# Attention on one core: probabilities transposed on TensorE, or a second score product with keys stationary

## Chip, core and metric

The kernel runs on one core of a Trainium2 chip. The metric is the device time of one execution in microseconds (us). The engines are TensorE (PE, with its weight loads listed as PEld), VectorE (DVE), ScalarE (ACT), GpSimd (POOL) and SyncE (SP), which issues nearly all transfers. Every engine takes its instructions in the order of its own list and waits at an instruction until what it needs is there.

## The reference, cut to what matters

```python
def _A_ref(x, wq, wk, wv, wo, beta):      # S = 2048, D = 1024, 32 heads of 32
    ...                                   # q, k, v: 4 segments of L = 512 rows
    for s in range(N):
        logits = jnp.einsum("bhqd,bhkd->bhqk", qs, ks) * scale + mask    # causal in a segment
        p = _softmax(logits, axis=-1)
        a_dot = jnp.einsum("bhqk,bhkd->bhqd", p, vs)
        num = jnp.einsum("bhld,bhde->bhle", pq, M)       # pq = phi(qs)
        den = jnp.einsum("bhld,bhd->bhl", pq, z)[..., None] + 1e-6
        o = g * num / den + (1.0 - g) * a_dot            # g = sigmoid(beta), by head
        M = M + jnp.einsum("bhld,bhle->bhde", pk, vs)    # pk = phi(ks)
        z = z + jnp.einsum("bhld->bhd", pk)
    return o @ wo
h = x + _A_ref(_layernorm(x), wq, wk, wv, wo, beta)
h2 = h + _B_ref(_layernorm(h), w1, b1, w2, b2)           # layernorm, dense, gelu, dense
```

## The kernel before, in words

All products keep near full single precision by splitting each factor into a high part, which TensorE multiplies in one pass, and a low part (`x = xh + xl`); three products `ah*bh + ah*bl + al*bh` make one (`mm3`, lines 124 to 126). A score product needs only one instruction, because the three blocks of 32 rows (high, low, high of the keys against high, high, low of the queries) lie under each other in a stack of 96 rows (`ks`, `qs`), which SP puts together by transfers (`stack`).

The program treats two halves of 1024 rows one after the other: attention with its three projections, then the product with `wo`, then the dense block. In a half there are two segments and eight groups of four heads. A **unit** is one group in one segment: `dense` projects keys, queries and values in 24 steps of three matmuls. Meanwhile `heads` treats the four heads of the unit before, six steps to a head; `interleave` takes the two in turn, one step each. 28 of the 32 units are in the steady stretch that the prediction speaks of.

What a head does at which step stands in the table `HEAD`: the number is the step, counted from the head's start (a head is 6 steps behind the one before it), the fraction orders what falls on the same step. `TIMES` does the same for the unit's own side work. This is the order in which the code is written out. A scheduler then makes each engine's list from it: it may move an instruction of lower rank ahead of one whose inputs or buffers it takes to be not yet ready. The lists below are its result.

For one head before:

- `qk`: four score products with a block of 128 queries stationary and 128, 256, 384 or 512 keys moving (`pqk`, line 659). DVE adds the mask, scales and takes the row's extreme in the same instruction, into `pr` and `mx` (line 660). ACT takes the exponential in place with the row's sum (line 668).
- `ptr`: ten transposes of 128x128 turn the probabilities so that keys lie on partitions (`ppt`, line 709), in groups of four, four and two. ACT makes the high part `pth` from each group (line 711), DVE the low part `ptl` (`sub`, line 716).
- `av`: eight products with 64 columns of values stationary, the high and low part of `v` side by side (`po`, line 729). ACT copies the low half out (`ot`, line 734), DVE adds the high half (line 740).
- `inverse` and `weigh`: reciprocals of the row sums, times 1 - g, for four heads at once; they are transposed (`pw`, line 688) and spread over partitions through DRAM (`r_dram`). POOL multiplies (`w`, line 743) and adds what the memory gave (line 747).

The banks of PSUM are shared out: two for scores (`qk`), two for transposed probabilities (`pt`), one for `po` (`av`), three for projections and the memory's products (`d`). POOL also makes the low parts of the weights (`wl`, line 799) and of `pk` and `pq`.

Of the kernel before, what the change touches and what calls it, by code (L numbers as in the profile page):

```python
# [17 lines left out]
P = 128  # L18
# [11 lines left out]
RA, RH, RS, PD, PS = 1.3, 14, 0.7, 20, 3  # L30
VT, KT, OT = True, True, True
WLC = 8
TIMES = dict(pk=10, kx=12, pkh=21, pkl=22, ks=11, qs=16, pq=16, pqh=20, pql=20, omt=20, vx=24, pm=25, vs=32, vl=33, pmm=40, om=35, omc=40, od=62, lk=13, lq=16, lv=20, ck=18, cq=22, cv=28)
HEAD = dict(r=6.1, q0=1.1, a0=14.1, s2=14.2, t0=8.3, q2=2.4, s0=8.5, a1=15.1, q1=3.2, t1=10.1, w=9.2, q3=4.3, t2=11.1, o=17.2, s1=11.3)
# [13 lines left out]
def build(tc, x, wq, wk, wv, wo, beta, w1, b1, w2, b2, out):  # L48
# [13 lines left out]
    hsel = const.tile([P, 76], F32, name="hsel")[:, 0:4]  # L62
# [6 lines left out]
    gate = const.tile([P, 2, H], F32, name="gate")  # L69
    bb = const.tile([P, H], F32, name="bb")  # L70
# [3 lines left out]
    def constants():  # L74
# [3 lines left out]
        nc.scalar.activation(gate[:, 1, :], gate[:, 0, :], AF.Identity, scale=-1.0, bias=1.0)  # L78
        pb = ps_dense("pb")
# [12 lines left out]
    r_dram = [dram.tile([16, P], F32, name=f"r_dram{k}") for k in range(2)]  # L92
# [260 lines left out]
    def attention(half, first):  # L353
# [6 lines left out]

        scr = [acts["zt"].tile([P, 4, 512], F32, tag=f"t{x_}3", name=f"sc{x_}") for x_ in "hl"]
# [31 lines left out]
        def stack(a, b, name, order):  # L393
            out = []
            n = acts[name] = acts.get(name, 0) + 1
            d = s_dram[name][n % 2]
            direct = {"ks": KD, "qs": QD}[name]
            for j in range(4):
                st = ab.tile([96, 512], F32R, tag=name, name=name, bufs=5)
                out.append(st)  # L400
                if j < direct:
                    for blk, src in enumerate(order):
                        nc.sync.dma_start(raw(st).rearrange("(r b) n -> b r n", b=3)[blk], raw((a, b)[src][32 * j:32 * j + 32, :]))
            if direct < 4:
                for blk, src in enumerate(order):
                    nc.sync.dma_start(d[32 * direct:, blk], raw((a, b)[src])[32 * direct:])
            for j in range(direct, 4):
                nc.sync.dma_start(raw(out[j]), d[32 * j:32 * j + 32].rearrange("r b n -> (r b) n"))
# [23 lines left out]
        def dense(g, sl, ws, u):  # L432
# [12 lines left out]
            vs = u["vs"] = ab.tile([P, 16, 64], F32R, name="vs", bufs=2)  # L445
# [11 lines left out]
            def key_stack():  # L457
                u["ks"] = stack(v["kh"], v["kl"], "ks", (0, 1, 0))
# [37 lines left out]
            def query_stack():  # L496
                u["qs"] = stack(v["qh"], v["ql"], "qs", (0, 0, 1))
# [183 lines left out]
        def weigh(st):  # L681
            u, j = st["u"], st["j"]
            if j < 3:
                return
# [917 lines left out]
```

## Time and profile before

| | |
|---|---|
| median of 3 runs | 2275.07 us (2273.71 to 2276.27) |
| span of the profiled execution | 2272.7 us |
| PE busy | 2243.7 us, 99% |
| DVE, ACT, POOL busy | 68%, 54%, 38% |
| attention and projections, first half | about 40 to 490 us of the span |
| the same, second half | about 900 to 1380 us |

The profiled execution is one run; its span goes from the first to the last instruction, and the median of the times is 2.4 us above that span. A row of the timeline gives the start, the duration, the engine, the line, the operation and the operands, and in brackets the idle time ahead of it. On PE, matmuls overlap: what one costs is the distance to the start of the next, not its duration. A row of the groups gives the count, then busy time and mean ns of one, then idle time before. In the source view the three numbers are the least, the median and the largest duration in ns. A row of the windows gives the stretch, its length, then the busy time (and count) of PE, PEld, DVE, ACT and POOL, the granted TensorE clock, the share of the DMA engines and GB/s.

### The profile page before, as it was taken

Reading aid. Unit: us, or ns where it says so; the run is one execution under the profiler, and the core shown is the slowest. Engines: PE = TensorE matmul, PEld = TensorE weight load, DVE = VectorE, ACT = ScalarE, POOL = GpSimd, SP = SyncE. Lnnn points to the kernel's source line nnn. Section 1 sums busy time; section 2 is a strip of 40 time slices with the busy share of each in tenths; the row PEclk is TensorE's granted clock in tenths of the full one; section 3 lists DMA queues with packets and bytes.
Section 4 is the critical chain, followed back from the end, with each engine's and each line's share of the span. In section 5 each row is a group of like instructions: output and inputs, shape, how many; then the busy total and the mean of one; then the engine's idle time right before and its main releaser. Section 6 shows DMA issues by size and latency. Waiting matters only on the chain.

```text
span 2272.7 us, 34849 instructions
## 1 busy us (share of the span) xinstructions
PE 2243.7 (99%) x11481; PEld 1861.9 (82%) x11481; DVE 1541.0 (68%) x3073; ACT 1232.8 (54%) x2553; POOL 856.8 (38%) x710
## 2 busy tenths in 40 slices
PE   8999999999999999999999999999999999999999
PEld 6888888877888888888888887888888888888887
DVE  6777777776656565777777787655666766567653
ACT  6777777774453445777777775453334223222221
POOL 4232233334244442233333334244445654055430
PEclk9999999999999999999999999999999999999999
DMA  6666666665475655666655565466568975476762
GB/s 215 182 190 181 181 179 176 177 177 196 139 212 165 189 167 173 195 177 179 178 173 169 178 195 189 142 210 181 162 177 310 331 253 197 155 257 226 244 234 89
DMA packets 400798, 437.41 MB, mean 192 GB/s; under 512 B 33102, under 2 KB 267114, under 8 KB 400618
## 3 DMA queue, kind: packets, MB, share of 16 engines
q1 hardware_dynamic: 337450, 398.48, 56.8%
q10 hardware_dynamic: 63168, 36.71, 5.4%
q8 instruction: 91, 1.49, 0.3%
q14 instruction: 89, 0.73, 0.1%
HBM read 287.41 MB, written 128.78 MB: 183 GB/s over the span
## 4 chain that ended last, share of the span: by engine, by line
PE 86%; DMA 4%; POOL 3%; ACT 2%; DVE 2%; issue 1%; SPq 1%; POOLq 0%; ACTq 0%; DVEq 0%
PE po L1436 22%; PE bps L1040 10%; PE cps L1040 7%; PE dps L1040 7%; PE po L729 6%; PE ppt L709 5%; PE pqk L659 3%; PE qps L124 3%; PE qps L125 2%; PE kps L124 2%; PE qps L126 2%; PE vps L124 2%; PE kps L126 2%; PE kps L125 2%; PE vps L125 2%; PE vps L126 2%
## 5 line engine op out<-in xcount | busy, mean ns | idle before, releaser
L668 ACT ACTIVATE pr<-pr,mx 128x128 f32<-128x128 f32 (+3 forms) x512 | 289.1, 565 | 107.3 <-DVE mx L660 104.0
L660 DVE CUSTOM_DVE_ANT_0 pr<-pqk,mask 128x128 f32<-128x128 f32 (+3 forms) x512 | 247.2, 484 | 87.0 <-PE pqk L659 82.2
L711 ACT CAST pth<-ppt 128x512 fp32r<-128x512 f32 (+1 forms) x384 | 194.9, 512 | 91.3 <-PE ppt L709 88.9
L716 DVE TENSOR_TENSOR ptl<-ppt,pth 128x512 fp32r<-128x512 f32 (+1 forms) x384 | 226.8, 595 | 14.5 <-ACT pth L711 11.9
L709 PE MATMUL ppt<-ident,pr 128*128 128x128 f32 x1280 | 217.4, 276 | 0.7 <-DVE ptl L716 0.4
L1446 DVE TENSOR_TENSOR c<-c,po 128x512 f32<-128x512 f32 x160 | 105.4, 683 | 149.0 <-PE po L1436 147.2
L709 PEld LDWEIGHTS ppt<-ident,pr 128*128 128x128 f32 x1280 | 163.9, 140 | 36.7 <-issue 2.2
L659 PE MATMUL pqk<-ks,qs 96*128 96x128 f32 (+3 forms) x512 | 183.0, 358 | 1.1 <-DVE mx L660 1.1
L799 POOL TENSOR_TENSOR wl<-wr,wh 128x1024 fp32r<-128x1024 f32 x42 | 101.1, 2406 | 179.1 <-ACT wh L797 132.0
L729 PE MATMUL po<-ptl,vs 128*64 128x512 f32 (+3 forms) x512 | 153.1, 308 | 1.9 <-DVE ptl L716 1.9
L729 PE MATMUL po<-pth,vs 128*64 128x512 f32 (+3 forms) x512 | 147.8, 309 | 2.9 <-DVE ot L740 1.6
L1436 PE MATMUL po<-w2h,zh 128*128 128x512 f32 x378 | 121.0, 390 | 0.2 <-DVE zh L1376 0.2
L1040 PE MATMUL bps<-zh,sb 128*128 128x512 f32 x336 | 111.1, 391 | 0.0
L1293 POOL TENSOR_TENSOR w2r<-w2r 128x512 f32<-128x512 f32 x54 | 85.4, 1590 | 68.3 <-DMA w2r<-in_B_w 45.4
L1040 PE MATMUL bps<-zh,sa 128*128 128x512 f32 x336 | 110.9, 391 | 0.0
L124 PE MATMUL kps<-yh,wh 128*128 128x512 f32 (+1 forms) x264 | 109.9, 416 | 0.0
L124 PE MATMUL qps<-yh,wh 128*128 128x512 f32 x256 | 107.8, 421 | 0.0
L124 PE MATMUL vps<-yh,wh 128*128 128x512 f32 x256 | 106.2, 415 | 0.0
L659 PEld LDWEIGHTS pqk<-ks,qs 96*128 96x128 f32 x512 | 98.2, 192 | 8.3 <-DVE mx L660 1.8
L1436 PE MATMUL po<-w2h,hl 128*128 128x512 f32 x322 | 103.3, 390 | 0.4 <-DVE hl L1376 0.4
L125 PE MATMUL kps<-yl,wh 128*128 128x512 f32 (+1 forms) x264 | 102.8, 389 | 0.1
L126 PE MATMUL kps<-yh,wl 128*128 128x512 f32 (+1 forms) x264 | 102.9, 390 | 0.0
(251 smaller groups left out, 6527.8 us busy)
## 6 DMA issues: line engine op xcount, KB each, us to landing
hr<-h_dram SPq DMA_DIRECT2D x112, 448.0 KB, 5.3
w2r<-in_B_w SPq DMA_DIRECT2D x122, 256.0 KB, 4.3
r<-in_B_w SPq DMA_DIRECT2D x56, 512.0 KB, 4.5
ks<-ks_dram SPq DMA_DIRECT2D x128, 192.0 KB, 3.1
h_dram<-ht ACTq DMA_DIRECT2D x84, 256.0 KB, 3.7
ks_dram<-kh SPq DMA_DIRECT2D x64, 256.0 KB, 2.6
wr<-in_A_wo SPq DMA_DIRECT2D x32, 512.0 KB, 4.5
wx<-in_B_w SPq DMA_DIRECT2D x56, 256.0 KB, 3.5
```

The lines of the kernel that those rows point to most:

```text
L124: nc.tensor.matmul(ps, ah, bh, start=first, stop=False)
L125: nc.tensor.matmul(ps, ah, bl, start=False, stop=False)
L126: acts["mm"] = nc.tensor.matmul(ps, al, bh, start=False, stop=last)
L659: nc.tensor.matmul(pqk[:, :n], u["qs"][j][:, i * P:(i + 1) * P], u["ks"][j][:, 0:n], start=True, stop=True)
L660: nc.vector.tensor_tensor_reduce(out=st["pr"][:, offs[i]:offs[i] + n], in0=pqk[:, :n], in1=mask[:, 512 - n:512], op0=ALU.add, op1=ALU.min, ...
L668: nc.scalar.activation(pi, pi, AF.Exp, bias=mx[:, i:i + 1], scale=-1.0, accum_out=mx[:, 4 + i:5 + i])
L709: nc.tensor.transpose(ppt[:, o:o + P], pr[:, offs[i] + jk * P:offs[i] + (jk + 1) * P], ident)
L711: acts["pth"] = n, nc.scalar.copy(pth[:, base:base + w], ppt[:, :w])
L716: nc.vector.tensor_tensor(o, x0, x1, op=ALU.subtract)
L729: nc.tensor.matmul(po[:, P * jk:], v, st[part][:, koff[jk]:koff[jk] + w], start=(jk, part) == (0, "pth"), stop=(jk, part) == (2, "ptl"))
L1040: nc.tensor.matmul(ps, x_[:, c, :], y_[:, c, :], start=first and c == 0 and n == 0, stop=last and c == 3 and n == 2, skip_group_check=True)
L1436: nc.tensor.matmul(ps, x_[:, k], y_[k], start=opens and k == 0 and i == 0, stop=closes and k == self.KP - 1 and i == 2, skip_group_check=True)
```

## The change

The transposes go. The scores are computed twice: the first product is there for the row's maximum alone; the second has the keys stationary, so that its result has keys on partitions at once. The maximum is taken off inside that second product: the query stack gets two more rows with the high and the low part of the maximum, the key stack two rows of -1. The path of the maximum is: DVE writes it as two parts into `top`, transposes 32x32 blocks into `mt`, SP stores that in DRAM (`top_dram`) and loads two rows of 512 into the stack (`rows`). ACT takes the exponential out of PSUM (`again`, `pe<-psc`), POOL zeroes the masked part of the diagonal blocks (`affine_select`), ACT makes the high part (`upper`), DVE the low part of 1024 columns and POOL that of the last 256 (`lower`). The values get a column of ones, so that row 64 of `po` is the row's sum; it goes out by `os` and through DRAM (`sums_dram`, `r_dram`). The stacks become six fixed buffers, the pipeline goes from two slots behind to four, and the tables of steps are new.

```diff
-HEAD = dict(r=6.1, q0=1.1, a0=14.1, s2=14.2, t0=8.3, q2=2.4, s0=8.5, a1=15.1, q1=3.2, t1=10.1, w=9.2, q3=4.3, t2=11.1, o=17.2, s1=11.3)
+HEAD = dict(q0=0.3, q2=1.2, q1=2.3, q3=3.3, x=4.1, y=6.6, p0=9.2, p1=10.2, p2=11.2, h0=11.4, h1=12.4, l0=12.3, l1=13.1, a0=15.1, a1=16.1, r=16.9,
+            o=18.2, v=19.2, i=21.4, d=21.6, w=23.8, e=26.4)
+RING = 6
...
+        values = [ab.tile([P, 16, 72], F32R, name=f"vs{n}") for n in range(2)]
+        for t in values:
+            nc.gpsimd.memset(raw(t[:, :, 64:65]), 1.0)
...
         def qk(st, i):
-            nc.tensor.matmul(pqk[:, :n], u["qs"][j][:, i * P:(i + 1) * P], u["ks"][j][:, 0:n], start=True, stop=True)
+            nc.tensor.matmul(pqk[:, :n], u["qs"][j][0:96, i * P:(i + 1) * P], u["ks"][j][0:96, 0:n], start=True, stop=True)
             nc.vector.tensor_tensor_reduce(
-                out=st["pr"][:, offs[i]:offs[i] + n], in0=pqk[:, :n], in1=mask[:, 512 - n:512],
-                op0=ALU.add, op1=ALU.min, scale=-SCALE, scalar=3.0e38, accum_out=st["mx"][:, i:i + 1])
-            soft(st, i)
-        def soft(st, i):
-            nc.scalar.activation(pi, pi, AF.Exp, bias=mx[:, i:i + 1], scale=-1.0, accum_out=mx[:, 4 + i:5 + i])
+                out=pqk[:, :n], in0=pqk[:, :n], in1=mask[:, 512 - n:512],
+                op0=ALU.add, op1=ALU.max, scale=1.0, scalar=-3.0e38, accum_out=st["mx"][:, i:i + 1])
...
+        def largest(st):
+            nc.vector.tensor_copy(top[:, 0:4], st["mx"])
+            nc.vector.tensor_tensor(top[:, 4:8], st["mx"], raw(top[:, 0:4]), op=ALU.subtract)
+            nc.vector.transpose(mt, raw(top))
+            BQ.dma_start(top_dram[n].rearrange("(z a r) -> a z r", a=4, r=32), mt)
+        def rows(st):
+            BQ.dma_start(raw(st["u"]["qs"][st["j"]][96:98, :]), st["top"][0:8 * P].rearrange("(p n) -> p n", p=2))
+        groups = ((0,), (1, 3), (2,))
+        def again(st, n):
+            ps = psum.tile([P, 512], F32, tag="pt", name="psc", bufs=2)
+            for jk in grp:
+                m = 512 - P * jk
+                nc.tensor.matmul(ps[:, w:w + m], u["ks"][j][0:98, jk * P:(jk + 1) * P], u["qs"][j][0:98, P * jk:],
+                                 start=True, stop=True)
+            pe = st["pe"][:, base:base + w]
+            nc.scalar.activation(pe, ps[:, :w], AF.Exp, scale=SCALE)
+            nc.gpsimd.affine_select(d, d, pattern=[[0, k]] * (k > 1) + [[1, P]], compare_op=ALU.is_ge, fill=0.0,
+                                    base=0, channel_multiplier=-1)
+        pieces = (slice(0, 1024), slice(1024, 1280))
+        def upper(st, n):
+            nc.scalar.copy(st["pth"][:, pieces[n]], st["pe"][:, pieces[n]])
+        def lower(st, n):
+            (nc.gpsimd if n else nc.vector).tensor_tensor(st["ptl"][:, c], st["pe"][:, c], raw(st["pth"][:, c]), op=ALU.subtract)
-        def ptr(st, n):
-                    nc.tensor.transpose(ppt[:, o:o + P], pr[:, offs[i] + jk * P:offs[i] + (jk + 1) * P], ident)
-            acts["pth"] = n, nc.scalar.copy(pth[:, base:base + w], ppt[:, :w])
-        def sub(st, n):
-            nc.vector.tensor_tensor(o, x0, x1, op=ALU.subtract)
...
         def av(st, n):
-                v = u["vs"][:, 4 * j + jk, :]
+                v = u["vs"][:, 4 * j + jk, 0:65]
-                nc.scalar.copy(u["ot"][32 * j:32 * j + 32, :], po[32:64, :])
+                nc.scalar.copy(st["os"][0:65, :], po[0:65, :])
+        def spread(st):
+            BQ.dma_start(sums_dram[u["n"]][j:j + 1, :], st["os"][64:65, :])
...
```

The names in the lists: `vps` and `qps` are projections, `psc` is a second score product, `pqk` a first one, `po` a product with the values. First PE, at the products with the values of one head (`po`) in the middle of the first half. Before:

```order
L729 MATMUL po<-pth,vs 64x512
L729 MATMUL po<-ptl,vs 64x512
L729 MATMUL po<-pth,vs 64x384
L729 MATMUL po<-ptl,vs 64x384
L709 MATMUL ppt<-ident,pr 128x128 x4
L659 MATMUL pqk<-ks,qs 128x384
L124 MATMUL vps<-yh_437,wh 128x512
L125 MATMUL vps<-yl_438,wh 128x512
L126 MATMUL vps<-yh_437,wl 128x512
L729 MATMUL po<-pth,vs 64x128
```

And now, in the same stretch of the program; the `psc` and the `po` in it belong to the same head:

```order
L726 MATMUL psc<-qs_513,ks_450 128x512
L726 MATMUL psc<-qs_513,ks_450 128x384
L726 MATMUL psc<-qs_513,ks_450 128x128
L694 MATMUL pqk<-stacks 128x128
L726 MATMUL psc<-qs_513,ks_450 128x256
L694 MATMUL pqk<-stacks 128x384
L694 MATMUL pqk<-stacks 128x256
L694 MATMUL pqk<-stacks 128x512
L759 MATMUL po<-pth,vs_367 65x512
L759 MATMUL po<-ptl,vs_367 65x512
L759 MATMUL po<-pth,vs_367 65x384
L759 MATMUL po<-ptl,vs_367 65x384
```

Before, a piece of a head is followed by three matmuls of a projection, all the way through, and the last transposes of a head stand eleven rows or more ahead of its first `po`. Now a head's `po` stand right behind its own `psc`, with no projection between, and the four `psc` and eight `po` of the next head come next; the projections stand together elsewhere. Second POOL, ahead of that same place. Before:

```order
L513 TENSOR_TENSOR pql<-pq,pqh 128x512
L569 TENSOR_TENSOR MZ<-MZ,hsel 128x128
L475 TENSOR_TENSOR pkl<-scl,pkh 128x512
L509 CAST mzh<-MZ 128x132
L510 TENSOR_TENSOR mzl<-MZ,mzh 128x132
```

And now:

```order
L865 TENSOR_TENSOR wl<-wr,wh 128x1024 x2
L605 TENSOR_SCALAR MZ<-MZ,zc 128x1
L606 TENSOR_SCALAR MZ<-hsel,MZ 128x4
L808 TENSOR_TENSOR sch<-ot,sch 128x512
L812 TENSOR_TENSOR sch<-sch,omt 128x512
L733 AFFINE_SELECT pe<-pe 128x128
L733 AFFINE_SELECT pe<-pe 128x2x128
L733 AFFINE_SELECT pe<-pe 128x128
L746 TENSOR_TENSOR ptl<-pe,pth 128x256
L865 TENSOR_TENSOR wl<-wr,wh 128x1024
```

POOL now has steps of a head's own chain in its list (`pe`, `ptl`), and the other work of the unit (`wl`, `sch`) stands ahead of them.

172 lines of the change are left out of this document (101 added, 71 removed).

## The prediction

> **What bounds the kernel now.** I read the page first.
>
> ```profile
> span 2272.7 us, 34849 instructions
> PE 2243.7 (99%) x11481; PEld 1861.9 (82%) x11481; DVE 1541.0 (68%) x3073; ACT 1232.8 (54%) x2553; POOL 856.8 (38%) x710
> ```
>
> PE is busy nearly all the time, but its ends are modelled, so I asked the windows for the two steady stretches of attention, and the groups of the first stretch for the number of heads in it.
>
> ```profile
> 60.00:480.00 420.00, 419.80 (x2519) 352.51 (x2519) 319.83 (x907) 321.75 (x807) 127.16 (x134) 1.00 0.63 181
> 900.00:1340.00 440.00, 439.22 (x2617) 367.61 (x2616) 337.66 (x973) 334.68 (x837) 140.82 (x138) 1.00 0.61 178
> ...
> L668 ACT ACTIVATE pr<-pr,mx 128x512 f32<-128x512 f32 x56 | 40.7, 726 | 10.0 <-DVE mx L660 9.4
> ```
>
> PE idles 0.2 of 420 us and 0.8 of 440 us, at full clock; DVE and ACT are busy three quarters of the time, POOL a third. 56 heads in 420 us are 7.5 us a head, 60 us for eight (two units). So the stretch goes at the pace of TensorE's list. A change there pays what it takes out of that list, as long as PE never has to wait; and any wait that it puts into the list costs its full length. The third view is the timeline of PE, for the price of each piece.
>
> ```profile
> 301.02 0.33 PE L729 MATMUL po<-pth,vs 128*64 128x384 f32 x1
> 301.19 0.34 PE L729 MATMUL po<-ptl,vs 128*64 128x384 f32 x1
> 301.37 0.60 PE L709 MATMUL ppt<-ident,pr 128*128 128x128 f32 x4
> 301.72 0.42 PE L659 MATMUL pqk<-ks,qs 96*128 96x384 f32 x1
> 301.98 0.40 PE L124 MATMUL vps<-yh,wh 128*128 128x512 f32 x1
> 302.22 0.40 PE L125 MATMUL vps<-yl,wh 128*128 128x512 f32 x1
> ...
> 302.74 0.22 PE L729 MATMUL po<-ptl,vs 128*64 128x128 f32 x1
> 302.80 0.28 PE L729 MATMUL po<-pth,vs 128*64 128x256 f32 x1
> 302.92 0.28 PE L729 MATMUL po<-ptl,vs 128*64 128x256 f32 x1
> ...
> 303.86 0.60 PE L709 MATMUL ppt<-ident,pr 128*128 128x128 f32 x4
> 304.21 0.48 PE L659 MATMUL pqk<-ks,qs 96*128 96x512 f32 x1
> 304.53 0.40 PE L124 MATMUL vps<-yh,wh 128*128 128x512 f32 x1
> 304.76 0.40 PE L125 MATMUL vps<-yl,wh 128*128 128x512 f32 x1
> ...
> 305.22 0.38 PE L709 MATMUL ppt<-ident,pr 128*128 128x128 f32 x2
> 305.36 0.48 PE L124 MATMUL kps<-yh,wh 128*128 128x512 f32 x1
> 305.68 0.39 PE L125 MATMUL kps<-yl,wh 128*128 128x512 f32 x1
> ```
>
> From start to start, 512 moving columns cost 0.23 us, 384 cost 0.17, 256 cost 0.12, 128 cost 0.06.
>
> **What TensorE gains.** The ten transposes of a head cost 0.35 + 0.35 + 0.14 = 0.84 us, and the instruction behind each of the three groups starts its successor 0.09 us late (0.26 for 0.17, twice 0.32 for 0.23): 1.11 us in all. The four new products have the widths 512, 384, 256 and 128: 0.58 us. That is 0.53 us a head, 68 us over 128 heads, all of it on the path. Two more rows in the stack and a 65th value column change no moving width; I take them as free.
>
> **What TensorE waits for.** Before, the transposes of a head lie well ahead of its products with the values, with projections between. In the new list those products come close behind the second scores, and PE cannot go on to anything else. Between them lies a chain over three engines, priced by the nearest rows:
>
> ```profile
> L384 ACT ACTIVATE e<-kps x24: 578/598/607, 28.1 to 1301.0; 128x512 f32<-128x512 f32 x24
> L345 POOL TENSOR_SCALAR_AFFINE_SELECT mask<-mask x2: 292/293/294, 1.7 to 887.8; 128x128 f32<-128x128 f32 x2
> L797 ACT CAST wh<-wr 128x1024 fp32r<-128x1024 f32 x13 | 13.6, 1050 | 4.8 <-DMA wr<-in_A_wv 3.4 <-PE kps L125 1.4
> L101 DVE TENSOR_TENSOR wl<-wr,wh x9: 1176/1226/2136, 464.8 to 1427.4; 128x1024 fp32r<-128x1024 f32 x9
> ```
>
> The first score product is through after 0.40 us; two exponentials out of PSUM take 0.60 us each; the select on two diagonal blocks lies between 0.29 us (one block) and 0.59 (two), I take 0.45; then the high part of 1024 columns, 1.05 us. So the first `po` can start 3.1 us after the first `psc`, or 2.5 us after the second one where that comes late. The second `po` needs the low part, 1.23 us on.
>
> What lies between in the list covers the wait. Priced by the widths above, the first half repeats this every eight heads: 1.2, 0.4 (counted from the second `psc`), 2.2, 4.7, 1.2, 0.6, 2.1 and 2.8 us of other PE work. The first of these is the place shown with the change: four `psc` and four `pqk`, 1.16 us. The waits left are 1.9, 2.1, 0.9, 0, 1.9, 2.5, 1.0 and 0.3, together 10.6 us. Between first and second `po` stand 0.5, 0.3, 1.2, 0.3, 0.2, 0.2, 1.4 and 1.2 us against 1.23; where the fourth head's low part was long ready, that leaves 3.6 us. That makes 14.2 us for eight heads; the second half's cadence (1.2, 0.4, 2.2, 2.7, 0.9, 2.7, 2.7, 0.6) gives 13.7 in the same way. 14 us, times 14 such cycles (112 heads; those at the start of a half are spaced more widely): 196 us. An error of 0.5 us in the chain moves it by some 45 us either way.
>
> Two queues lengthen this chain.
>
> ```profile
> L743 POOL TENSOR_TENSOR sch<-ot,sch 128x512 f32<-128x512 f32 x7 | 9.1, 1299 | 7.1 <-DMA sch<-r_dram 4.8 <-DVE ot L740 2.3
> L747 POOL TENSOR_TENSOR sch<-sch,omt 128x512 f32<-128x512 f32 x7 | 9.2, 1319 | 0.5
> L660 DVE CUSTOM_DVE_ANT_0 pr<-pqk,mask 128x128 f32<-128x128 f32 (+3 forms) x512 | 247.2, 484 | 87.0 <-PE pqk L659 82.2
> L740 DVE TENSOR_TENSOR ot<-po,ot 32x512 f32<-32x512 f32 x57 | 38.7, 679 | 13.0 <-ACT ot L734 12.2
> ```
>
> On POOL the selects stand behind the unit's last multiply and add, 2.6 us that wait for a transfer: once in eight heads up to 2.6 us, or nothing if the transfer is early; I take 1. On DVE, once in eight heads the first products of four heads stand within 8.1 us of PE work, while their row maxima take 16 x 0.48 = 7.7 us and five operations like `ot` among them 3.4: about 3 us late, part of which lies in waits already counted; I take 2, between 0 and 5. Together 3 x 14 = 42 us. DVE's own load hardly changes: three low parts become one of 1.23 us, and three small operations on four columns come in. ACT loses four exponentials and gets three, so it has time. The low part now reads two SBUF tiles while POOL works: the row's largest, 2.14 us, bounds that. With it, the four heads per cycle that wait for the low part would lose 0.9 us each, 50 us in all. The Trainium skill (GPSIMD Engine Reference, Specifications) says that POOL shares its SBUF interfaces with VectorE and contends with DVE instructions of two SBUF inputs; by that rule the 50 us would come on top, 2530. The median in the row, taken beside a busy POOL, speaks for little of it.
>
> The pipeline's end is two slots longer; other work is there for PE, so I take 10 us, between 0 and 40.
>
> **The clock.** The one place of the trace where PE waits a little is the end of the first half:
>
> ```profile
> 488.00:491.50 3.50, 3.50 (x30) 3.16 (x29) 2.27 (x7) 1.64 (x4) 0.00 (x0) 1.00 0.75 227
> ...
> 509.40:512.80 3.40, 1.61 (x12) 0.98 (x10) 2.49 (x8) 3.35 (x8) 2.12 (x1) 1.00 0.03 7
> 512.80:516.30 3.50, 3.21 (x8) 2.54 (x9) 1.32 (x1) 0.12 (x2) 0.24 (x1) 0.51 0.56 154
> ...
> 511.24 0.45 PE L729 MATMUL po<-pth,vs 128*64 128x512 f32 x1 [0.91 <-DVE ot L740]
> ...
> 513.09 0.79 PE L125 MATMUL pwo<-zl,oh 128*128 128x512 f32 x1 [1.18 <-POOL zl L101]
> ```
>
> After 3.4 us with PE busy for 1.6, the next 3.5 us run at half clock, though no single gap was longer than 1.2 us. The new list has two such clusters in each cycle. Each could lose up to 1.7 us; about half of that time PE would be waiting anyway. 28 x 0.85 = 24 us, between 0 and 95. The Trainium skill (TensorE: Matmul & The Clock Gate, Why this matters for your kernels) asks only that no PE-idle gap exceed about 3 us; by that rule none of these waits would cost clock, and the sum would be 24 us less. The trace disagrees: gaps of 0.91 and 1.18 us sufficed.
>
> **The sum.** -68 + 196 + 42 + 10 + 24 = +204 us on the profiled execution's 2272.7: 2476.7. The median lies 2.4 us above that span, which makes 2479 us.
>
> **Rivals.**
>
> *TensorE's gain decides, faster.* If the chain behind the second scores were covered, the 68 us would remain: 2207 us. The point from which it decides is a wait of 4.9 us in eight heads (68 / 14) instead of 14. For it speaks that ACT is relieved, and that the trace shows no PE wait under a fuller ACT. Against it: one exponential alone takes half of what covers most of these places. Chance 0.08, and 0.03 for a balance within 0.2%, which is about what a measurement of this kernel can tell from no change.
>
> *The clock falls in every cluster, and PE's work lies in the slow time.* 95 us instead of 24: 2550. The windows above show how little is needed; against it, waiting time costs nothing at half clock. Chance 0.15.
>
> *SP becomes the bound.* The two maximum rows go through SP's queue, behind everything else that it issues.
>
> ```profile
> L403 SPq DMA_DIRECT2D qs<-qh x192: 506/588/1727, 34.3 to 1345.8; - x192
> ...
> r_dram<-scl SPq DMA_DIRECT2D x16, 8.0 KB, 2.9
> ```
>
> The new list has 53 issues in a unit instead of 40. At up to 0.59 us that is 31 us, and four times the load of the rows waits for a store just ahead of it to land (2.9 us, less what is issued meanwhile, say 2): 39 us. The forecast's unit takes 30 us, less 2 of gain, plus 7 of waits, 1.5 of queues and 1 of clock, 37.5. It would need more than that to decide; with each wait at its full 2.9 us it is 43, and 28 x 5 = 140 us more, 2620. For it: the queue holds the loads of the stacks, which wait for PE, ahead of the rows. Against it: most issues take 0.3 to 0.45. Chance 0.10.
>
> *The new products cost more than their widths*, so that nothing is gained on PE: 2547 us; it shares the chance of the forecast, 0.64.
>
> **How the numbers follow.** The likeliest case gives 2479 us. Its own bounds come from the chain (45 us either way), the queues (0 to 106), the pipeline's end and the clock: roughly 2390 to 2600. The range reaches to 2360, for the chain and the queues both at their low ends, and to 2640, which takes in the clock and SP; outside are the faster case and the worst of SP. Slower: 0.64 + 0.15 + 0.10 = 0.89; same 0.03; faster 0.08.
>
> **What would show it.** The profile after should have PE well below 99% in the two attention stretches, around 80%, with idle time ahead of `po<-pth` and `po<-ptl` put down to ACT and DVE; a half-clock share in the row of the granted clock; DVE and ACT no fuller than before; about 75 us for eight heads. If PE is still at 99% there, the chain is covered and I am wrong. If its waits lie ahead of `psc` and end with a transfer, it was SP.

## The result, and the profile after

The changed kernel takes 2732.43 us (median of 4 runs, 2729.37 to 2737.67) against 2275.62 us of the kernel before on the same chip: 1.2014 times as long, with an interval of 1.1996 to 1.2032. It is slower by 457 us where +204 was forecast, and lies outside the range. The page of the profile after, its head and the row of the granted clock:

```profile
span 2732.5 us, 33546 instructions
PE 2450.9 (90%) x10681; PEld 1921.7 (70%) x10681; DVE 1627.2 (60%) x3141; ACT 1080.1 (40%) x1753; POOL 1158.5 (42%) x1210
PEclk9987889898799999998888888789999999999999
```

The windows of three consecutive stretches of eight heads in the first half:

```profile
312.30:401.10 88.80, 72.47 (x310) 53.49 (x310) 49.45 (x133) 36.42 (x65) 36.56 (x49) 0.85 0.42 120
401.10:489.90 88.80, 72.29 (x310) 53.42 (x310) 49.50 (x133) 36.42 (x65) 36.60 (x49) 0.87 0.43 120
489.90:578.60 88.70, 71.75 (x307) 53.00 (x306) 49.39 (x132) 36.63 (x65) 36.61 (x49) 0.85 0.42 120
```

Eight heads take 88.8 us where they took 60 and 75 were forecast; 14 times 28.8 us is 403 of the 457. PE idles some 16.4 us of them. If all the lost clock was lost at half speed (0.51 in the prediction's window), a mean of 0.85 means some 27 us at half clock, an estimate. ACT and DVE are less busy than before, 41% and 56% where they were at 76%. The waits of the whole span name those two engines all the same, ahead of `psc` and `po`:

```profile
L726 PE MATMUL psc<-qs,ks 98*128 98x512 f32 (+3 forms) x432 | 134.0, 393 | 38.3 <-ACT pe L730 34.0
L759 PE MATMUL po<-pth,vs 128*65 128x512 f32 (+3 forms) x512 | 182.1, 378 | 69.1 <-ACT pth L742 62.2
L759 PE MATMUL po<-ptl,vs 128*65 128x512 f32 (+3 forms) x512 | 183.6, 384 | 37.1 <-DVE ptl L746 30.6
L746 DVE TENSOR_TENSOR ptl<-pe,pth 128x1024 fp32r<-128x1024 f32 x128 | 171.0, 1336 | 166.5 <-ACT pth L742 166.0
L730 ACT ACTIVATE pe<-psc 128x512 f32<-128x512 f32 (+1 forms) x384 | 187.4, 525 | 172.5 <-PE psc L726 112.0
```

So PE waits for ACT and DVE, DVE for ACT, ACT for PE, and none of them is full. A chain that starts late can look like that. SP's own queue shows where. Its waits between 150 and 450 us:

```profile
SPq L771 <- ACT os L765: 63.0, 20, 4.8
SPq L823 <- POOL pe L733: 33.0, 4, 8.3
SPq L787 <- DVE rs L783: 13.2, 4, 4.7
```

SP stands 109 of 300 us at three stores: the sums of a head (for ACT's copy of `po`), the output of a unit (for POOL) and the inverses (for DVE). One of the four longest of these waits (8.0 to 8.3 us) in the timeline of SP, with the transfers around it:

```profile
335.93 0.24 SPq L712 DMA_DIRECT2D qs<-top_dram  x1
336.22 0.30 SPq L442 DMA_DIRECT2D qs<-qs_dram  x1
336.62 0.40 SPq L857 DMA_DIRECT2D wr<-in_A_wv  x1
337.07 0.57 SPq L708 DMA_DIRECT2D top_dram<-mt  x1
340.36 0.23 SPq L771 DMA_DIRECT2D sums_dram<-os  x1
348.59 0.34 SPq L823 DMA_DIRECT2D o_dram<-sch  x1
348.98 0.42 SPq L402 DMA_DIRECT2D turn_dram<-sch  x1
349.50 0.28 SPq L712 DMA_DIRECT2D qs<-top_dram  x1
```

The maximum of the next head was stored at 337.07; its two rows are loaded at 349.50. In between SP waits 2.7 us to store the sums, and then 8.0 us to store an output that is read only towards the end of this half's attention. POOL's timeline over the same time tells why the output is late, and the windows what the rest did meanwhile:

```profile
345.27 0.30 POOL L605 TENSOR_SCALAR MZ<-MZ,zc 128x1 f32<-128x1 f32 x1 [12.25 <-DVE pk L424]
345.66 0.30 POOL L606 TENSOR_SCALAR MZ<-hsel,MZ 128x4 f32<-128x4 f32 x1
345.93 1.28 POOL L808 TENSOR_TENSOR sch<-ot,sch 128x512 f32<-128x512 f32 x1
347.28 1.28 POOL L812 TENSOR_TENSOR sch<-sch,omt 128x512 f32<-128x512 f32 x1
```

```profile
340.60:348.60 8.00, 7.08 (x36) 5.36 (x34) 7.06 (x26) 2.34 (x5) 3.12 (x4) 1.00 0.00 1
348.60:357.00 8.40, 5.14 (x16) 3.19 (x16) 7.01 (x18) 5.06 (x10) 5.48 (x7) 0.71 0.39 128
```

POOL stood 12 us at a small operation of the memory's update that waited for DVE. The multiply and the add behind it (L808, L812) came late, SP's output store waited for them, and for 8 us no transfer moved (DMA share 0.00). PE used up its projections in that time; afterwards it is busy for 5.14 of 8.40 us, at clock 0.71, with little but score products and the late chain. So far this reading is a conjecture: the kernel before also has SP waiting, 104 us in the same 300, without harm. The experiments decide.

### The profile page after: what moved, and what is told of

Read it like the earlier page. It is cut to its first block, busy times and chain, and to the rows that moved or that the text cites. A ratio compares the mean times of both kernels' runs of the same rounds, so it can differ in the third digit from the quotient of the medians.

```text
span 2732.5 us, 33546 instructions
## 1 busy us (share of the span) xinstructions
PE 2450.9 (90%) x10681; PEld 1921.7 (70%) x10681; DVE 1627.2 (60%) x3141; ACT 1080.1 (40%) x1753; POOL 1158.5 (42%) x1210
## 3 DMA queue, kind: packets, MB, share of 16 engines
q1 hardware_dynamic: 363306, 401.63, 47.9%
## 5 line engine op out<-in xcount | busy, mean ns | idle before, releaser
L695 DVE CUSTOM_DVE_ANT_0 pqk<-pqk,mask 128x128 f32<-128x128 f32 (+3 forms) x512 | 248.7, 499 | 162.6 <-PE pqk L694 157.1
L733 POOL TENSOR_SCALAR_AFFINE_SELECT pe<-pe 128x128 f32<-128x128 f32 (+1 forms) x384 | 130.1, 351 | 371.6 <-ACT pe L730 371.0
L746 DVE TENSOR_TENSOR ptl<-pe,pth 128x1024 fp32r<-128x1024 f32 x128 | 171.0, 1336 | 166.5 <-ACT pth L742 166.0
L730 ACT ACTIVATE pe<-psc 128x512 f32<-128x512 f32 (+1 forms) x384 | 187.4, 525 | 172.5 <-PE psc L726 112.0
L759 PE MATMUL po<-pth,vs 128*65 128x512 f32 (+3 forms) x512 | 182.1, 378 | 69.1 <-ACT pth L742 62.2
L746 POOL TENSOR_TENSOR ptl<-pe,pth 128x256 fp32r<-128x256 f32 x128 | 164.8, 1287 | 132.8 <-ACT pth L742 125.5
L759 PE MATMUL po<-ptl,vs 128*65 128x512 f32 (+3 forms) x512 | 183.6, 384 | 37.1 <-DVE ptl L746 30.6
L742 ACT CAST pth<-pe 128x1024 fp32r<-128x1024 f32 (+1 forms) x256 | 174.3, 724 | 45.2 <-POOL pe L733 39.7
L726 PE MATMUL psc<-qs,ks 98*128 98x512 f32 (+3 forms) x432 | 134.0, 393 | 38.3 <-ACT pe L730 34.0
L759 PEld LDWEIGHTS po<-ptl,vs 128*65 128x65 f32 x512 | 85.6, 170 | 95.1 <-DVE ptl L746 58.9
L726 PEld LDWEIGHTS psc<-qs,ks 98*128 98x128 f32 x432 | 94.8, 232 | 70.5 <-ACT pe L730 54.4
```

The source lines that it names most:

```text
L695: nc.vector.tensor_tensor_reduce(out=pqk[:, :n], in0=pqk[:, :n], in1=mask[:, 512 - n:512], op0=ALU.add, op1=ALU.max, scale=1.0, scalar=-3. ...
L726: nc.tensor.matmul(ps[:, w:w + m], u["ks"][j][0:98, jk * P:(jk + 1) * P], u["qs"][j][0:98, P * jk:], start=True, stop=True)
L730: nc.scalar.activation(pe, ps[:, :w], AF.Exp, scale=SCALE)
L733: nc.gpsimd.affine_select(d, d, pattern=[[0, k]] * (k > 1) + [[1, P]], compare_op=ALU.is_ge, fill=0.0, base=0, channel_multiplier=-1)
L742: nc.scalar.copy(st["pth"][:, pieces[n]], st["pe"][:, pieces[n]])
L746: (nc.gpsimd if n else nc.vector).tensor_tensor(st["ptl"][:, c], st["pe"][:, c], raw(st["pth"][:, c]), op=ALU.subtract)
```

## The experiments

**First round: is it PE's list?** The forecast blamed the products that the scheduler put close behind the second scores. Four kernels test that. `pin_pe` holds PE's list to the written order; `pin_all` holds all five; `warm5` gives PE five more 512-column products per head between second scores and values, as filler; `low_dve` takes the last low part off POOL.

```diff
+    @contextmanager
+    def pinned(*engines):          # afterwards: each instruction of these engines behind the one written before it
+        ...
-                    interleave(d, heads(prev), 1.0)
+                    with pinned(mybir.EngineType.PE):
+                        interleave(d, heads(prev), 1.0)
```

> The changed kernel, with TensorE's list of the 30 interleaved units held to the order in which the code is written (steps of HEAD, evenly spaced), and nothing else changed. If the bunching of second scores and value products in TensorE's list made the waits, and the waits the half clock, TensorE is busy over 95% of the attention stretches at full clock and the time falls below that of before: 2275 - 68 + some 30 for what is left of waits, 2240 us (2200 to 2330). If a queue (the maximum rows through SP, POOL's selects) is the bound whatever TensorE's order, it stays above 2600 us and the waits only move.

> The same, with the lists of all five engines held to the written order. If bunching on TensorE was the cause, within 2% of the run with TensorE alone held (2190 to 2330 us). If SP's or POOL's list is what matters, this one is clearly faster than that one, or, if the written order puts a store and the load behind it too close, clearly slower.

```diff
+                for _ in range(5):             # warm5: ahead of the first product with the values
+                    op = nc.tensor.matmul(po[0:65, :], y[:, 1, 0:65], y[:, 0, :], start=True, stop=True)
```

> The changed kernel with five extra products of 512 columns (results overwritten) put into TensorE's list behind the second scores of each head, ahead of its value products: 5 x 0.23 = 1.2 us of work a head, 150 us in all at full clock, put where TensorE waits about 2 us. The waits themselves stay. If the half clock carries about half of the loss (27 us of half clock in a cycle of eight heads), its share falls and the time goes down in spite of the added work, to 2500 to 2650 us. If the half clock costs nothing because it lies in the waits, the time stays at 2730 or rises by up to 100 us.

```diff
-            (nc.gpsimd if n else nc.vector).tensor_tensor(st["ptl"][:, c], ...)
+            nc.vector.tensor_tensor(st["ptl"][:, c], ...)       # low_dve
```

> The changed kernel with the low part of the last 256 columns on DVE instead of POOL; TensorE's list is as bunched as before. On POOL that piece takes 1.29 us, as long as the low part of 1024 columns on DVE beside it, so it may be held up by DVE. If bunching is the cause, the change is small: 2690 to 2750 us. If POOL's delay carries the loss, 2600 us or less.

| kernel | us, median (range) | against before | mean clock |
|---|---|---|---|
| pin_pe | 2713.63 (2711.32 to 2715.36) | 1.1928 [1.1911, 1.1946] | 0.934 |
| pin_all | 3145.33 (3141.72 to 3151.68) | 1.3834 [1.3807, 1.3862] | 0.875 |
| warm5 | 2720.82 (2711.39 to 2727.15) | 1.1957 [1.1927, 1.1987] | 0.953 |
| low_dve | 2720.01 (2718.22 to 2722.34) | 1.1958 [1.1940, 1.1975] | 0.919 |

My theory fell. With PE's list in the written order the kernel is 19 us faster, not 450. 640 extra products, some 150 us of work at 0.23 us each, do not cost time but go with 12 us less. The clock rises with them, over the span from 0.917 to 0.953, and in the four stretches of 100 us from 1200 us on from at most 0.85 to at least 0.98. So neither PE's work nor its clock sets the time. POOL's low part is worth 12 us. But holding PE's list shows what is late. The two largest of PE's waits in `pin_pe`, for the whole span:

```profile
PE psc L741 <- DMA qs<-top_dram: 278.0, 50, 11.5
PE po L774 <- DVE ptl L761: 28.5, 29, 1.8
```

In the written order PE meets the second scores first, and waits for the two rows of the maximum, up to 11.5 us at a time. One of these waits, 11.3 us until 288.69 us, has this on SP meanwhile (some rows):

```profile
272.02 1.21 SPq L451 DMA_DIRECT2D qs<-qh  x2
277.17 0.36 SPq L802 DMA_DIRECT2D r_dram<-rs  x1
282.87 0.59 SPq L723 DMA_DIRECT2D top_dram<-mt  x1
286.24 0.24 SPq L727 DMA_DIRECT2D qs<-top_dram  x1
```

From 272.02 to 281.26 us SP issues the nine loads of a query stack, 5.3 us of issues, with one wait of 3.0 us for the inverses among them. Only then does it store the maximum, and six other issues later it loads the rows. So the rows stand behind issues as well as behind waits. The scheduler's list of the changed kernel puts projections into these gaps; PE waits there only 2.3 us for the rows. That the same delay comes out further down, as waits for ACT and DVE, is an inference from the two lists. In `pin_all` PE's waits for the rows grow to 393.0 us (`qs`) and 117.9 us (`stacks`), which goes with its being so much slower.

**Second round: SP's queue.** Four edits, each to the changed kernel alone.

```diff
-            o=18.2, ... a1=16.1, r=16.9
+            o=18.2, ... a1=16.1, r=18.8                        # sums_later: after the next rows' load
-    BQ, TQ, LQ, OQ = nc.sync, nc.sync, nc.sync, nc.sync
+    BQ, TQ, LQ, OQ = nc.scalar, nc.sync, nc.sync, nc.sync      # max_act: BQ is maximum, sums, weights
-HEAD = dict(..., x=4.1, y=6.6, ...)
+HEAD = dict(...)                                               # no_top: no store, no load of the maximum
-                        nc.sync.dma_start(raw(out[j][0:96, :])...
+                        nc.scalar.dma_start(raw(out[j][0:96, :])...   # qs_act: nine loads of a query stack
```

> The store of a head's sums stands in the written order just ahead of the next rows' load; here it comes two steps later (r = 18.8 for 16.9), so that the scheduler can put it behind that load; nothing else is changed. Theory 1 (SP's queue sets the pace: the sums' store waited 303 us in all for the copy of the products, and the rows' load and everything else stood behind it): that wait no longer delays the rows, 100 to 200 us less, 2530 to 2630 us. Theory 2 (the length of the chain over ACT, POOL and DVE sets the pace, SP has slack): unchanged, 2715 to 2750 us.

> The DMAs of the maximum, the sums and the weights are issued by ACT, 18 in a unit; the stacks, the turned tiles and the loads stay on SP. Theory 1 (SP's queue): the rows no longer stand behind nine stack loads of 0.59 us and other transfers; ACT is 40% busy and pays about 18 x 0.37 = 7 us a unit: 2450 to 2600 us. Theory 2 (the chain's length): nothing won on SP, and the exponentials and casts stand behind ACT's waits for the maxima: 2750 to 2900 us.

> Leaves the maximum's way out: the two rows are zero all the time, no copy of the maxima, no store and no load of the rows (the maximum is not subtracted); the sums and everything else stay. If the way of the maximum through SP and DRAM sets the pace, its 8 issues in a unit, the wait for the landing of the store (about 2 us) and the order behind the sums go: 14 x 2 units lose about 8 to 12 us each, 2400 to 2500 us. If the chain from the second scores to the values sets the pace, the time stays within 2680 to 2740 us.

> The nine direct loads of the query stack in each unit are issued by ACT instead of SP, 9 x 0.59 us less for SP and about 9 x 0.37 us more for ACT; the maximum stays on SP. If the number of issues on SP is the bound: up to 5.3 us a unit, 32 units, 2560 to 2620 us. If SP's waits and not its issues bind: 2700 to 2740 us; if ACT then waits for the query halves: up to 2800 us.

| kernel | us, median (range) | against before | to the changed kernel |
|---|---|---|---|
| sums_later | 2742.32 (2740.30 to 2743.68) | 1.2058 [1.2040, 1.2076] | +10 |
| max_act | 2478.96 (2477.59 to 2482.03) | 1.0905 [1.0887, 1.0923] | -253 |
| no_top | 2576.52 (2573.97 to 2580.55) | 1.1331 [1.1312, 1.1351] | -156 |
| qs_act | 2548.69 (2542.78 to 2549.82) | 1.1202 [1.1183, 1.1221] | -184 |

The same transfers on another queue, and 253 us are gone. The windows of `max_act` over two of its units:

```profile
280.00:350.00 70.00, 62.50 (x316) 48.74 (x316) 52.77 (x135) 37.85 (x67) 36.58 (x52) 0.98 0.54 155
```

Eight heads in 70 us instead of 88.8, at clock 0.98, with about the same number of matmuls. `qs_act` moves no part of the maximum, and gains 184 us; so it is not the maximum's transfers as such, but how long everything stands in one line. Nine issues of 0.59 us a unit are 149 us in 28 units and 170 in all 32, most of this gain. By my own ranges that speaks for the number of issues; SP's waits alone were to leave 2700 us or more. `no_top`, which subtracts no maximum, fell between its two ranges. `sums_later` missed the range by which SP's queue sets the pace, and fell into that of the rival, by which SP has slack. SP's largest waits of that kernel between 150 and 450 us show why it need not speak for the rival:

```profile
SPq L787 <- DVE rs L783: 47.9, 7, 7.9
SPq L823 <- POOL pe L733: 23.0, 4, 7.6
SPq L771 <- ACT os L765: 20.8, 10, 4.3
```

The wait for the sums fell from 63.0 to 20.8 us; the wait for the inverses, which come from these sums, rose from 13.2 to 47.9. Within one queue the wait changed its place.

**Third round: what is left with the maximum on ACT.** All four are `max_act` with one more edit.

```diff
+                        nc.scalar.dma_start(raw(out[j][0:96, :])...   # both_act: nine loads of a query stack too
+                    with pinned(mybir.EngineType.PE):                  # max_act_pin
-            nc.gpsimd.affine_select(d, d, ...)                         # max_act_nosel: no select
+                        nc.gpsimd.dma_start(raw(out[j][0:96, :])...   # qs_pool: those nine on POOL
```

> The DMAs of the maximum, the sums and the weights and also the nine direct loads of the query stack are issued by ACT; SP keeps the key stack, the turned tiles, the weight loads and the outputs. If SP's queue still binds after either move alone (2479 and 2549 us): 2380 to 2440 us. If with the maximum on ACT the rest of the loss is the chain and the order on PE: 2460 to 2500 us.

> The maximum, the sums and the weights on ACT's queue, and PE's list held to the written order, where the products with the values stand six steps behind the second scores. Theory A (with SP out of the way the rest of the loss is the bunched order on PE, as the forecast had it): 2250 to 2350 us. Theory B (the order on PE does not matter, something else is late): 2450 to 2500 us. Theory C (PE's written order is worse where the transfers come late): above 2500 us.

> The maximum, the sums and the weights on ACT's queue, and the two selects of a head on POOL are left out (the upper triangle of the diagonal blocks is not masked), so that the high part follows the exponentials directly. If the chain from the second scores to the values is what is left of the loss: about 0.45 us and two hand-overs less in every head, 128 x 0.5 = 64 us, 2400 to 2430 us. If something else is: 2460 to 2485 us.

> The maximum, the sums and the weights on ACT's queue, the nine direct loads of the query stack on POOL's. If SP's queue still binds: below 2440 us. If ACT's time was the limit of the kernel that has both on ACT, this one is the faster of the two. If POOL's selects then stand behind the loads' wait for the query halves: 2500 us or more.

| kernel | us, median (range) | against before | to max_act |
|---|---|---|---|
| both_act | 2602.36 (2599.61 to 2606.07) | 1.1446 [1.1427, 1.1465] | +123 |
| max_act_pin | 2531.84 (2530.17 to 2533.86) | 1.1131 [1.1114, 1.1147] | +53 |
| max_act_nosel | 2432.38 (2431.28 to 2435.64) | 1.0695 [1.0679, 1.0711] | -47 |
| qs_pool | 2501.32 (2499.93 to 2513.47) | 1.1008 [1.0979, 1.1036] | +22 |

Moving more transfers off SP no longer helps, on ACT or on POOL; `both_act` lies above both of its ranges. Nothing here says that SP still binds, but the engines that take the transfers pay as well. On ACT they hurt, as two rows of ACT's timeline in `both_act` show:

```profile
332.71 0.60 ACTq L436 DMA_DIRECT2D qs<-ql  x1
333.36 0.58 ACT L765 COPY os<-po 65x512 f32<-65x512 f32 x1 [5.02 <-DMA qs<-qh]
```

ACT's copy stood 5.0 us behind ACT's own issues. The written order on PE is again not the cure (+53 us). Without the selects 47 us go, which takes a link out of the chain from the second scores to the values, and work off POOL.

**Fourth round: which of SP's transfers, and how much chain.** The first three kernels move only a part of SP's transfers to ACT in the changed kernel; the other three go on from `max_act`.

```diff
+    BQ, TQ, LQ, OQ = nc.sync, nc.sync, nc.sync, nc.scalar     # out_act: the unit's output alone
+    BQ = nc.scalar, but top_dram and the rows on nc.sync      # sums_act
+    BQ = nc.sync, but top_dram and the rows on nc.scalar      # rows_act
+            nc.vector.tensor_tensor(st["ptl"][:, c], ...)      # max_act_low: max_act, whole low part on DVE
+    BQ, TQ, LQ, OQ = nc.scalar, nc.sync, nc.sync, nc.scalar   # act_low: max_act_low and the output
+            st["pth"], st["ptl"] = fixed                       # cut: max_act without casts and low parts
```

> Only the store of a unit's attention output to DRAM is issued by ACT, one issue in a unit; everything else stays on SP. Theory Q (what holds up the rows is SP's waits for work that is done late, here 33 us in 300 us of the first half for POOL's multiply and add of the unit's end): up to 3.5 us a unit for 28 units, 2630 to 2690 us. Theory N (the number of issues is what counts): 0.4 us a unit, 2715 to 2735 us. If ACT now waits in place of SP and the casts stand behind it: above 2735 us.

> The sums' stores, their load, the store of the inverses and the four loads of the weights (10 issues in a unit) are issued by ACT; the two DMAs of the maximum stay on SP. Theory Q: the waits for the copy of the products (63 us in 300) and for the inverses (13) go, 2500 to 2580 us, near the kernel that moves the maximum too. Theory N: 10 of 53 issues, about 4 us a unit of SP's time, 2620 to 2680 us.

> Only the two DMAs of the maximum in each head (8 issues in a unit) are issued by ACT; the sums, the weights and the output stay on SP with their waits. If it matters that the rows stand behind SP's other transfers and waits: 2480 to 2560 us, though SP still waits as long. If the stacks, which stay behind these waits, are as late as the rows: 2600 to 2700 us.

> The maximum, the sums and the weights on ACT's queue, and the low part of the last 256 columns on DVE (about 0.4 us) instead of POOL (1.29 us, behind the cast and beside the selects). If the chain behind the second scores is what is left: 0.9 us less at its far end, which only the last two products see, and the selects stand behind nothing of it: 2430 to 2465 us. If DVE, which is at 74% there, then is late with the maxima: 2480 to 2510 us.

> The maximum, the sums, the weights and the output store on ACT's queue, and the whole low part on DVE. If the output store's wait still delays the stacks and turned tiles on SP: 10 to 45 us less than without it, 2420 to 2455 us. If SP no longer sets anything: 2460 to 2470 us; if ACT then stands in the wait for POOL: above 2475 us.

> The maximum, the sums and the weights on ACT's queue. The high and low parts of the probabilities are left out: the products with the values read two constant tiles, so that they wait for no exponential, select, cast or subtraction; the second scores, the exponentials and the selects are still run, and PE has the same products. If the gain of 0.53 us a head on PE holds and the chain is all that is left: 2207 us and some 10 to 30 for the rest, 2207 to 2240 us. If the products on PE cost about what the transposes did: 2265 to 2300 us. If waits for the maxima and their rows keep PE idle even so: above 2300 us.

| kernel | us, median (range) | against before | |
|---|---|---|---|
| out_act | 2684.92 (2683.09 to 2688.86) | 1.1803 [1.1783, 1.1822] | -48 to the changed kernel |
| sums_act | 2612.63 (2610.16 to 2615.38) | 1.1488 [1.1471, 1.1505] | -120 to the changed kernel |
| rows_act | 2651.48 (2645.82 to 2658.27) | 1.1659 [1.1633, 1.1686] | -81 to the changed kernel |
| max_act_low | 2466.93 (2462.23 to 2473.37) | 1.0849 [1.0826, 1.0871] | -12 to max_act |
| act_low | 2476.92 (2466.86 to 2482.94) | 1.0870 [1.0835, 1.0904] | +10 to max_act_low, ranges overlap |
| cut | 2398.89 (2397.16 to 2402.39) | 1.0539 [1.0523, 1.0554] | -80 to max_act |

`out_act` separates issues from waits. It moves one issue of 0.34 us in a unit, 28 x 0.34 = 10 us of SP's time, and gains 48. What else it takes from SP is the wait in front of that issue; the wait for the sums grows meanwhile, from 63.0 to 79.9 us in the 300. The Trainium skill (DMA: Bandwidth & Descriptors, Issuing engines are not separate DMA queues) says that issuing from several engines saves only the time that the sequencer takes to start the transfer; by that the gain would end at 10 us, and the measurement speaks against it: the second queue also saves what stands behind a wait. The sums with the inverses and the weights are worth 120 us, the maximum 81, both together 253, so the parts do not add up. `sums_act` fell between its two ranges; `rows_act` fell into the one for stacks that are as late as the rows. So each alone seems to leave its share behind the same stack loads, which no run separates. With both away, the output store makes no difference that these runs can tell (`act_low`).

`cut` shows how much the chain can be worth once the 18 transfers are off SP: at most 80 us, since the casts and low parts also leave their engines. ACT is busy for 25.6 us of a stretch where `max_act` above has 37.9, DVE for 41.8 where it has 52.8. `cut` also shows what else is there. Its windows over four times two units, and the largest of its PE waits between 150 and 450 us:

```profile
205.70:272.00 66.30, 58.09 (x307) 47.32 (x306) 41.09 (x125) 24.91 (x49) 24.97 (x41) 0.97 0.58 161
272.00:339.40 67.40, 58.37 (x313) 47.35 (x314) 42.66 (x126) 26.32 (x52) 25.14 (x42) 1.00 0.54 156
339.40:406.30 66.90, 58.27 (x307) 47.28 (x306) 41.52 (x125) 24.91 (x48) 25.65 (x42) 0.97 0.56 161
406.30:475.00 68.70, 60.70 (x311) 49.57 (x311) 41.84 (x126) 26.05 (x51) 26.00 (x43) 0.95 0.54 155
sum 269.30, PE 235.42 PEld 191.52 DVE 167.11 ACT 102.19 POOL 101.77; mean PE 58.86 PEld 47.88 DVE 41.78 ACT 25.55 POOL 25.44
```

```profile
PE psc L726 <- ACT pe L730: 9.7, 8, 1.6
PE pqk L694 <- DVE mx L695: 9.2, 6, 2.1
PE psc L726 <- DMA stacks<-top_dram: 6.4, 3, 3.4
PE psc L726 <- DMA qs<-top_dram: 6.2, 4, 2.8
```

With no chain in front of the values PE still idles 8.5 of 67.3 us in the mean, as much as in `max_act` (7.5 of 70): ahead of `psc`, for ACT's exponentials, which empty the two PSUM buffers, and for the rows, and ahead of `pqk`, for DVE's maxima. Here 123 us over the kernel before remain. So of the 457 us, 253 go with the 18 transfers, 80 more with the chain and the work in it, and no run removed the other 123. No version that I ran beats the kernel before.

## Why the prediction was wrong, step by step

**The sign and the signs in the profile came true; the cause did not.** I had written that PE would be at about 80% in attention, idle ahead of `po` for ACT and DVE, with a half-clock share, DVE and ACT no fuller. PE is at 82% and the rest holds too. But these signs do not tell my theory from the rival: a chain that starts late looks the same from PE as a chain that is too long. The sign that I had named for SP (waits ahead of `psc` that end with a transfer) is 2.3 us in the changed kernel and 298 us in `pin_pe`, where PE's list is held.

**The step that failed is the price of the rival "SP becomes the bound", which stands at nothing in the forecast's sum.** The runs put 253 of the 457 us there. The rival had the right queue, and the stack loads ahead of the rows, with a chance of 0.10 and 2620 us. It summed 53 issues at up to 0.59 us (31 us) and 8 us of waiting for the store of the maximum to land, 39 us a unit. Added up over the timeline of SP between 150 and 450 us, 354 issues took 165 us, 0.47 us each, or 24.4 us in a unit of 44.4. All its waits there were 123 us, 18 us a unit. So issues were priced too high and waits at less than half; and the waits were of another kind. The load of the rows hardly waited for the landing: its line is not among SP's waits between 150 and 450 us, and over the whole span, with 128 such loads, it has this row:

```profile
SPq L712 <- DMA top_dram<-mt: 3.8, 4, 1.5
```

What SP waited for was other engines' work: the copy of `po`, the inverses, the unit's multiply and add. I had said in the part on queues that POOL's multiply and add wait for a transfer, and never asked who waits for POOL.

The comparison itself was wrong too. I held the queue's total against the length of a unit, but SP is always issuing or waiting. In the kernel before, 409 issues took 195 us of the same 300 and waits 104, with PE never idle. What the runs point to is how late the rows and stacks come: they stand behind nine stack loads in one run (`qs_act` gains 184 us) and behind waits for ACT, DVE and POOL (`out_act` gains 48).

By the written order the new transfers close a loop: the rows stand behind the sums, the sums behind the values, the values behind the rows of two heads before. That this loop sets the pace is not shown. `sums_act` opens it and gets 120 of the 253 us back, and `pin_pe`, where SP waits for the copy of `po` for 5.2 us between 150 and 450 us instead of 63.0, is nearly as slow as the changed kernel.

**TensorE's gain was counted too high.** In the four stretches of `cut` shown above, PE is busy 58.9 us for eight heads, against 60.0 before. Taking the half-clock time off (mean clock 0.972, 1.9 us) leaves 57.0. So 1.1 to 3.0 us are gained where 4.2 were forecast. Successors of `psc` start late too, which the forecast had only for the transposes: between 200 and 340 us of `cut`, a projection product of 512 columns behind a `psc` costs 0.24 to 0.28 us at the median, by kind of projection, against 0.23 behind one of its own kind and 0.32 behind the transposes before.

**The waits behind the bunched list (196 us)** are real, but smaller. `cut` puts the whole chain at 80 us at most with the 18 transfers off SP; leaving out the selects alone gains 47. Nothing shows that the bunching makes them: holding PE's list to an order with more distance made `max_act` slower by 53 us, not faster. My 14 us for eight heads assumed that everything ahead of the chain is on time. (The 3.6 us among them add up to 3.8 from the figures given, some 3 us of the 196.)

**The queues on POOL and DVE (42 us)**: these were not measured by themselves. The low part's move off POOL gains 12 us in either setting, and the selects' time on POOL is in the 47 us above. POOL's late multiply also acts through SP, 48 us, which was not in the sum.

**The clock (24 us)** fell far more than I took, some 27 us at half clock in eight heads where two clusters of 3.5 us were foreseen. It cost little that can be seen: `warm5` raised it for a gain of 12 us at most. The forecast was right that waiting time costs nothing at half clock, and wrong to put 24 us on the path. **The pipeline's end (10 us)** was not tried.

That `max_act` lands on 2479 us, the very forecast, is no support for the sum. It has 70 us for eight heads where the forecast had 75, and its parts are other ones. **What stays open** is how the 253 us divide between the stacks' delay and the rows' delay, and between issues and waits; whether transfers on ACT's queue also land sooner (the views of the changed kernel give no time from issue to landing); and what sets the last 123 us of `cut` (PSUM buffers, maxima, rows), which these runs show as waits but do not separate.

## What to carry to other kernels

When a change sends a per-head result through memory and back on a queue that other work shares, do not hold the queue's total against the length of the loop. For each new transfer, ask what stands in front of it: how many issues in a row, and which engine's late result they wait for. Ask also whether the transfer stands behind work that it releases itself. If the waits of the profile go round between engines of which none is full, hold the busiest engine's list to a fixed order for one run, and move a single suspect transfer to another queue: the first shows what comes late in that order, and the gain of the second against its issue time tells the wait from the issue.

## What the runs showed of the hardware beyond that

The low part of 256 columns on POOL and that of 1024 columns on DVE in the changed kernel: the durations over all heads (least, median, largest ns), then two places of the timelines.

```profile
L746 POOL TENSOR_TENSOR ptl<-pe,pth x128: 722/1458/1798, 61.1 to 1828.1; 128x256 fp32r<-128x256 f32 x128
350.96 0.73 POOL L746 TENSOR_TENSOR ptl<-pe,pth 128x256 fp32r<-128x256 f32 x1 [1.22 <-ACT pth L742]
351.07 1.70 DVE L746 TENSOR_TENSOR ptl<-pe,pth 128x1024 fp32r<-128x1024 f32 x1
357.99 1.23 DVE L746 TENSOR_TENSOR ptl<-pe,pth 128x1024 fp32r<-128x1024 f32 x1 [1.60 <-ACT pth L742]
358.34 1.46 POOL L746 TENSOR_TENSOR ptl<-pe,pth 128x256 fp32r<-128x256 f32 x1 [1.01 <-ACT pth L742]
```

And a copy of four columns on DVE, with one of the longest beside a subtraction on POOL:

```profile
L704 DVE CAST top<-mx x128: 127/170/2105, 44.3 to 1782.4; 128x4 fp32r<-128x4 f32 x128
351.91 3.10 POOL L865 TENSOR_TENSOR wl<-wr,wh 128x1024 fp32r<-128x1024 f32 x1 [0.21 <-ACT wh L863]
352.93 2.10 DVE L704 CAST top<-mx 128x4 fp32r<-128x4 f32 x1
```

- Of POOL's and DVE's subtractions, the one that starts second is held up. Between 60 and 640 us POOL's takes 0.73 to 0.74 us where it starts first or alone (13 times). Where DVE's started first (40 times), it takes 1.47 us in the mean and ends 0.59 us behind DVE's. The Trainium skill (GPSIMD Engine Reference, Specifications) has POOL and VectorE share their SBUF interfaces and contend where DVE reads two SBUF inputs. The trace agrees. POOL mostly pays for it, since DVE mostly starts first; with the low part off POOL, DVE's subtraction takes 0.02 us less in the mean (`low_dve`, 1.316 for 1.336 us), not the 0.9 us that I had bounded it by.
- A copy of four columns takes 0.17 us on DVE at the median, and up to 2.1. In the same stretch, each of the 12 that took over 0.3 us lies beside a POOL operation of two inputs and ends within 0.04 us of its end.
- The clock fell for nearly a third of a stretch of eight heads (mean 0.85) although PE was busy for 82% of it. Lifting it gained 12 us at most, because PE was not what the end waited for.
